# Top-32 attention and two MLPs on one core: both heads' masks on ScalarE in the first 20 attention steps, with a new set of order priorities

## The chip, the cores and the metric

One core of one Trainium2 chip runs the whole program. The metric is the device time of one execution, in microseconds. The kernel before has a median of 669.65 us over three runs (668.49 to 670.56). The engines are called PE (TensorE, the matmuls), PEld (TensorE's weight loads), DVE (VectorE), ACT (ScalarE), POOL (GpSimd) and SP (SyncE, which issues every DMA here).

## The reference, cut to what matters

```python
def _attn_ref(q, k, v):                  # q, k, v: (2, 8, 576, 64)
    scores = scale * np.matmul(q, k.transpose(0, 1, 3, 2))
    kth = np.partition(scores, -32, axis=-1)[..., -32:-31]
    scores = np.where(scores >= kth, scores, -1e9)
    scores = scores - np.max(scores, axis=-1, keepdims=True)
    attn = np.exp(scores)
    attn = attn / (np.sum(attn, axis=-1, keepdims=True) + 1e-09)
    return np.matmul(attn, v)

def _moe_ref(x, w_in, w_out):            # x: (1152, 512), d_ff 2048
    h = x @ w_in
    return (h * np.tanh(softplus(h))) @ w_out

def _moe2_ref(x, w_a, w_b, w_out):       # d_ff 1536
    return ((x @ w_a) * (x @ w_b)) @ w_out
```

The attention's output (1152 tokens by 512) goes through the first MLP and that through the second. Of each row of 576 scores only those that reach the 32nd largest count.

## The kernel before, in words

**Tiles and steps.** The 1152 tokens are nine tiles of 128, t = 0 to 8. Attention takes a tile in four steps (`hp` = 0 to 3, two heads each), 36 steps in all, in the order t, hp. Step number 4t + hp runs through these lines:

- `scores` (L405): q is split into two fp32r parts (`cast` L338, `minus` L343), PE multiplies (L420), and ACT scales the result into the score tile `s2` (L425).
- `largest` (L429): four rounds on DVE for each of the two heads. Each round finds the next eight largest values of 576 (MAX8, L439), and all but the last strike them out (MATCH_REPLACE8, L443). POOL makes `nm`, minus the largest value, after round one (L448).
- `weighted_sum` (L452): the masked exponentials `e2` and their row sums `sm`. The two heads go two ways. Head 0: ACT takes exp(score + nm) (L464), and DVE multiplies that by score >= kth with one SCALAR_TENSOR_TENSOR that also gives the row sum (L467). Head 1: POOL forms `dm` = kth + nm (L471), ACT takes a Prelu of kth - score with slope 2 to the -100 below zero (L474), and ACT takes exp of minus 2 to the 100 times that plus `dm`, with the row sum (L477); what lies below kth comes out as zero.
- PE transposes `e2` in three groups of three (L487), ACT copies them (L338), PE multiplies by v (L499, L503), and ACT copies the result.
- In a tile's last step (hp = 3) the row sums are inverted (L514, L516), spread by PE (L522), and multiplied in by DVE (L528). That gives the tile's `X`.

**MLPs.** `SEQ` (L26) gives their order: the first MLP for tile 0, 1 and 2 alone with f32 matmuls, the second MLP for tiles 0 to 2 together, then first and second for tiles 3 to 5, and first and second for tiles 6 to 8, with operands split in two fp32r parts. In `gated` (first MLP, L642) PE makes a block of h (L595), DVE and ACT make the gate (L670, L675, L678), PE accumulates (L616, L618). In `bilinear` (second MLP, L709) ACT copies one product, DVE multiplies (L725), PE accumulates (L618).

**Weights.** The weights come as 64-bit words in 68 units. Each unit is loaded, turned to fp32 by two ACT instructions (L546, L549) and two POOL instructions (L556, L560), stored to DRAM (`ws`) and read again by later users (`weight`, L567).

**Order.** Every operation is added to a `Plan` (L62) with the engines that may run it, a cost in ns and a priority. `Plan.run` (L108) is a list scheduler: it steps through its own clock, and each engine takes the ready operation of the lowest priority number whose buffers are free. The program is then emitted in that order, so on the chip each engine has a fixed order of instructions. The priority numbers come from tables: `ATT` (a knot for each attention tile), `CONV` (weights), `MLP` (a pair for each entry of `SEQ`) and `BIAS` (an offset for each kind of operation). Casts may go to ACT or DVE and subtractions to POOL or DVE (`SHIFT` adds to an engine's priority for them); `LOCKED` charges an operation for waiting on a lock that the planner assumes between DVE and POOL.

Of the kernel before, what the change touches and what calls it, by code (L numbers as in the profile page):

```python
# [9 lines left out]
F32 = mybir.dt.float32  # L10
F32R = mybir.dt.float32r
I32 = mybir.dt.int32
U32 = mybir.dt.uint32
AF = mybir.ActivationFunctionType
ALU = mybir.AluOpType
# [3 lines left out]
P = 128  # L19
U = 512  # L20
TOPK = 32
F1, F2 = 16, 12
NEG = -3.0e38
STEEP = 2.0 ** 100

SEQ = [(1, (0,), 0), (1, (1,), 0), (1, (2,), 0), (2, (0, 1, 2), 1), (1, (3, 4, 5), 1), (2, (3, 4, 5), 1),  # L26
       (1, (6, 7, 8), 1), (2, (6, 7, 8), 1)]
ATT = (-44.2, 61.0, 80.2, 153.1, 238.0, 259.3, 281.3, 398.4, 274.4, 469.0)
CONV = (-27.3, 62.1, 145.7, 238.5, 305.1)
MLP = ((99.9, 149.6), (74.9, 213.2), (116.2, 202.1), (235.2, 335.9), (398.3, 83.3), (374.8, 661.3), (641.9, 1133.6),  # L30
        (636.8, 878.2))
BIAS = {'scores': -33.7, 'search': 20.5, 'weigh': 16.8, 'gate': -247.0, 'conv': 3.7, 'load': -25.3, 'split': -20.8,
        'x': -50.1, 'k': -24.9, 'prod': -14.5, 'acc': 7.3, 'out': -497.1, 'store': 13.6, 'v': 290.8, 'px': 5.6,
        'mask': 2.0, 'turn': -2.6}
FRESH = 200
KEEP = (1, 1, 1, 1, 1, 3, 3, 3)
AHEAD = 1500.0
SLACK = 2500.0
ISSUE = 430.0
TICK = 3413.0  # L40
DUTY = 0.375
SPARE = (6000.0, 4000.0, 3000.0, 2000.0, 1000.0, 500.0, 0.0)
# [219 lines left out]


LAG = {"PE": 200.0, "DVE": 135.0, "ACT": 150.0, "POOL": 110.0, "SP": 2200.0}
SHIFT = {'DVE': 20.6, 'POOL': -2.0, 'ACT': 198.1, 'PE': 0, 'SP': 0}
LOCKED = 85.8


def ramp(knots, z):
# [6 lines left out]
def topk_attention_mlps(ctx: ExitStack, tc: tile.TileContext, q, k, v, vr, w, out):  # L276
# [5 lines left out]

    nc = tc.nc
    B, D, H, S = k.shape
    DM = H * D
    NC = DM // P
    NP = H // 2
    J = 4
    SM = J * P
    R = S - SM  # L290
# [8 lines left out]
    add = plan.add  # L299
# [3 lines left out]
    def buf(pool, shape, dtype, name, cap=1):  # L303
        if pool == "dp":
            return plan.buf(lambda b: pools[pool].tile(shape, dtype, name=name), None, 0)
        n = (8 if dtype == mybir.dt.int64 else 4)
        for z in shape[1:]:
            n *= z

        def make(b):  # L310
            a = arena[b.kind][:shape[0], b.at // 4:(b.at + n) // 4]
            if dtype != b.kind:
                a = a.bitcast(dtype)
            if len(shape) > 2:
                dims = "abcde"[:len(shape) - 1]
                a = a.rearrange(f"p ({' '.join(dims)}) -> p {' '.join(dims)}", **dict(zip(dims, shape[1:])))
            return a
        b = plan.buf(make, None if pool == "const" else f"{pool}.{name}", cap)
        b.size, b.kind, b.name = -(-n // 32) * 32, F32R if dtype == F32R else F32, name
        return b  # L320
# [7 lines left out]
    def one(engine, cost, locks=False):  # L328
        return {engine: (cost, locks)}
# [23 lines left out]
    nc.vector.memset(eight, 8)  # L353
    nc.scalar.preload_act_table_set("natural_log_exp_and_others")

    V, V4, KK, QQ, X, XR, Y = {}, {}, {}, {}, {}, {}, {}

    def groups(t):
        return [(t // (J + 1), 0, P)] if t != J else [(b, b * R, R) for b in range(B)]
# [66 lines left out]
                    [(psc, 0)], [(s2, (s, a))])  # L426
        return s2

    def largest(s2, at):  # L429
        pr = at + BIAS["search"]  # L430
        wk, m8 = buf("att", [P, 2, S], F32, "wk", CAPS["wk"]), buf("att", [P, 2, TOPK], F32, "m8", 2)
        nm = buf("att", [P, 2], F32, "nm", 2)
        for r in range(TOPK // 8):
            for s in range(2):
                src = wk if r else s2
                keys = [(wk, s)] if r else [(s2, (s, a)) for a in range(2)]
                got = slice(8 * r, 8 * r + 8)
                add(one("DVE", 672.0), pr,
                    lambda e, s=s, src=src, got=got: nc.vector.max(m8()[:, s, got], src()[:, s, :]),  # L439
                    keys, [(m8, (s, r))])  # L440
                if r < TOPK // 8 - 1:
                    add(one("DVE", 680.0), pr,
                        lambda e, s=s, src=src, got=got: nc.vector.match_replace(wk()[:, s, :], m8()[:, s, got],  # L443
                                                                                src()[:, s, :], NEG),
                        keys + [(m8, (s, r))], [(wk, s)])
            if r == 0:
                add(one("POOL", 174.0), pr,
                    lambda e: nc.gpsimd.tensor_scalar(nm(), m8()[:, :, 0], -1.0, None, op0=ALU.mult),  # L448
                    [(m8, (0, 0)), (m8, (1, 0))], [(nm, 0)])
        return m8, nm  # L450

    def weighted_sum(t, hp, at, s2, m8, nm):  # L452
        pr = at + BIAS["weigh"]
        if hp == 0:
            if t in (0, J):
                load_v(t // J, pr + BIAS["v"])
            XR[t] = buf("att", [P, NP, P], F32, "xr", 2), buf("att", [P, H], F32, "sm", 2)
        xr, sm = XR[t]
# [1 line left out]
        last = TOPK // 8 - 1  # L460
        kth = lambda s: m8()[:, s, TOPK - 1:TOPK]
        at_ = lambda s: sm()[:, 2 * hp + s:2 * hp + s + 1]
        s0, s1 = ([(s2, (s, a)) for a in range(2)] for s in range(2))
        add(one("ACT", 665.0), pr, lambda e: nc.scalar.activation(e2()[:, 0, :], s2()[:, 0, :], AF.Exp,  # L464
                                                                bias=nm()[:, 0:1]), s0 + [(nm, 0)], [(e2, 0)])
        add(one("DVE", 740.0, True), pr + BIAS["mask"],
            lambda e: nc.vector.scalar_tensor_tensor(e2()[:, 0, :], s2()[:, 0, :], kth(0), e2()[:, 0, :],  # L467
                                                   op0=ALU.is_ge, op1=ALU.mult, accum_out=at_(0)),
            s0 + [(m8, (0, last)), (e2, 0)], [(e2, 0), (sm, (hp, 0))])
        dm = buf("att", [P, 1], F32, "dm", 2)  # L470
        add(one("POOL", 142.0), pr, lambda e: nc.gpsimd.tensor_add(dm(), kth(1), nm()[:, 1:2]),  # L471
            [(m8, (1, last)), (nm, 0)], [(dm, 0)])
        add(one("ACT", 665.0), pr,
            lambda e: nc.scalar.activation(e2()[:, 1, :], s2()[:, 1, :], AF.Prelu, scale=-1.0, bias=kth(1),  # L474
                                           alpha=1.0 / STEEP), s1 + [(m8, (1, last))], [(e2, 1)])
        add(one("ACT", 775.0), pr,
            lambda e: nc.scalar.activation(e2()[:, 1, :], e2()[:, 1, :], AF.Exp, scale=-STEEP, bias=dm(),  # L477
                                           accum_out=at_(1)), [(e2, 1), (dm, 0)], [(e2, 1), (sm, (hp, 1))])
        et = buf("att", [P, 2 * J + 1, P], F32, "et", CAPS["et"])
        for g in range(3):  # L480
            pe = bank("pe")
# [50 lines left out]
    for t, hp in steps:  # L532
        at = ATT[t] + (ATT[t + 1] - ATT[t]) * hp / NP
        s2 = scores(t, hp, at)
        weighted_sum(t, hp, at, s2, *largest(s2, at))

    order = [(z, f, i) for z, F in ((0, F1), (1, F2)) for f in range(F) for i in range(2 + z)]
    stored, fresh = {}, {}
# [100 lines left out]
            add(one("DVE", 600.0), pr, lambda e: nc.vector.tensor_sub(put(yl), src(), put(yh).bitcast(F32)),  # L639
                read + [(yh, i)], [(yl, i)])  # L640

    def gated(z, tiles, split, yt, places, direct):  # L642
        n = len(tiles)
        T = n * P
        base = lambda f: MLP[z][0] + (MLP[z][1] - MLP[z][0]) * f / F1
# [6 lines left out]
            xz = [((X[tiles[0]], 0), lambda c: X[tiles[0]]()[:, c, :])]  # L652
        acc = [bank("acc", "ps_a") for _ in tiles]
        if direct:
            acc.append(bank("acc"))
        K = WIDE.get(T, 1)
        for f0 in range(0, F1, K):
            ph = bank("ph", "ps_h")
# [24 lines left out]
                add_product(base(f0 + j), acc, gj, wb, n, f0 + j == 0, f0 + j == F1 - 1, direct)  # L683
        pr = base(F1)
        if direct:
            for c in range(NC):
                put = lambda y, c=c: y()[:, c, :]
                add(one("ACT", 75.0 + 0.83 * T), pr + BIAS["x"],
                    lambda e, c=c, put=put: nc.scalar.mul(put(yt[0]), acc[c]()[:, :T], -1.0), [(acc[c], 0)],
                    [(yt[0], c)])  # L690
                add(one("DVE", 65.0 + 1.04 * T), pr + BIAS["x"],
                    lambda e, c=c, put=put: nc.vector.scalar_tensor_tensor(
                        put(yt[1]), acc[c]()[:, :T], -1.0, put(yt[0]).bitcast(F32), op0=ALU.mult, op1=ALU.subtract),
                    [(acc[c], 0), (yt[0], c)], [(yt[1], c)])
            return
        for i in range(n):
            y = buf("xp", [P, DM], F32, "y")
            add(one("ACT", 495.0), pr + BIAS["x"], lambda e, y=y, i=i: nc.scalar.mul(y(), acc[i](), -1.0),
                [(acc[i], 0)], [(y, 0)])
            pt = bank("pt")  # L700

            def turn(e, y=y, pt=pt):
                for c in range(NC):
                    nc.tensor.transpose(pt()[:, c * P:(c + 1) * P], y()[:, c * P:(c + 1) * P], ident)

            add(one("PE", 440.0), pr + BIAS["x"], turn, [(y, 0)], [(pt, 0)])
            parted(pr, lambda pt=pt: pt().rearrange("p (c t) -> p c t", t=P), [(pt, 0)], yt, places[i], False)

    def bilinear(z, tiles, yt):  # L709
        n = len(tiles)  # L710
# [30 lines left out]
    for i, (kind, tiles, split) in enumerate(SEQ):  # L741
        if kind == 2:
            bilinear(i, tiles, Y[tiles[0]][0])
            continue
        if tiles[0] not in Y:
            group = next(z[1] for z in SEQ if z[0] == 2 and tiles[0] in z[1])
            yt = [buf("xp", [P, NC, len(group) * P], F32R, f"y{z}{len(group) * P}", CAPS["y"]) for z in "hl"]
            Y.update({t: (yt, j) for j, t in enumerate(group)})
        whole = any(z[0] == 2 and z[1] == tiles for z in SEQ)
        gated(i, tiles, split, Y[tiles[0]][0], [Y[t][1] for t in tiles], i == final and split and whole)  # L750

    started = plan.run()
    plan.place(started, ROOM)
# [49 lines left out]
```

## Time and profile before

| what | value |
|---|---|
| median of three runs | 669.65 us (668.49 to 670.56) |
| the profiled execution's own time | 669.99 us |
| its span, from first to last instruction | 668.2 us |
| PE busy | 612.0 us, 92% of the span |
| PEld busy | 538.5 us, 81% |
| DVE busy | 583.8 us, 87% |
| ACT busy | 479.6 us, 72% |
| POOL busy | 403.6 us, 60% |
| mean granted TensorE clock | 0.977 of full speed |

The shares are averages over stages that differ. The profile lists the busy time of each engine in stretches of the span, the chain of work that ended last, each line's instructions with their mean duration, and who waited for whom. PE's busy time is modelled, so a busy PE need not be a PE at its peak.

### The profile page before, as it was taken

The page shows a single profiled execution, that of the slowest core. Times are in us where ns is not written, and L with a number is a line of the kernel's source. Part 1 is how long each engine was busy: PE and PEld are TensorE (multiplying, and loading weights), DVE is VectorE, ACT ScalarE, POOL GpSimd, SP SyncE. Part 2 cuts the span into 40 slices and gives each one's busy share as a digit, 9 for nine tenths or more (in the row PEclk, how much of TensorE's full clock was granted, in tenths as well). Part 3 has the DMA queues.
Part 4 walks back from the last instruction along what each step waited for, and adds up shares of the span by engine and source line. Part 5 has one row for each costly group of instructions (what it writes and reads, how often), then busy time and mean ns, then how long its engine had stood idle before and what let it go on. Part 6 is the DMA issues. An engine that isn't in the chain of part 4 may idle for free.

```text
span 668.2 us, 12021 instructions
## 1 busy us (share of the span) xinstructions
PE 612.0 (92%) x4000; PEld 538.5 (81%) x4000; DVE 583.8 (87%) x1141; ACT 479.6 (72%) x1040; POOL 403.6 (60%) x417
## 2 busy tenths in 40 slices
PE   1567987799989999999999999899999999999997
PEld 1455965677775989887799998899899999999997
DVE  4999999999999999999999999999973676675661
ACT  4789988869878798989799876766663687632222
POOL 5898867457559899999987656375631122321220
PEclk9958998999999999999999999999999999999999
DMA  9978886996999968777564433232304544444401
GB/s 268 301 246 266 223 258 162 339 337 202 336 334 285 304 191 267 239 229 242 177 199 145 127 103 118 80 80 80 110 1 150 182 136 134 126 127 127 128 14 47
DMA packets 55869, 123.99 MB, mean 186 GB/s; under 512 B 7424, under 2 KB 7424, under 8 KB 55808
## 3 DMA queue, kind: packets, MB, share of 16 engines
q1 hardware_dynamic: 55808, 123.23, 59.6%
q8 instruction: 31, 0.51, 0.3%
q14 instruction: 30, 0.25, 0.1%
HBM read 103.02 MB, written 20.19 MB: 184 GB/s over the span
## 4 chain that ended last, share of the span: by engine, by line
PE 54%; DVE 18%; DMA 4%; ACT 3%; POOL 3%; issue 3%; SPq 0%; DVEq 0%; POOLq 0%; ACTq 0%
PE ph L595 28%; PE po L618 8%; DVE arena L439 7%; PE acc L618 5%; DVE arena L443 5%; PE acc L616 5%; PE px L499 3%; DMA arena<-ws 2%; PE pe L487 2%; PE psc L420 2%; DMA ws<-arena 2%; POOL arena L560 1%; DVE arena L467 1%; DVE arena L343 1%; ACT arena L338 1%
## 5 line engine op out<-in xcount | busy, mean ns | idle before, releaser
L343 POOL TENSOR_TENSOR arena<-arena,arena 128x512 fp32r<-128x512 f32 (+4 forms) x186 | 217.8, 1183 | 178.4 <-ACT arena L338 155.6
L595 PE MATMUL ph<-arena 128*128 128x384 f32 (+1 forms) x1632 | 284.5, 324 | 8.2 <-POOL arena L560 4.8
L595 PEld LDWEIGHTS ph<-arena 128*128 128x128 f32 x1632 | 264.1, 189 | 24.0 <-issue 10.3
L439 DVE MAX8 arena<-arena 128x8 f32<-128x576 f32 x288 | 204.7, 746 | 0.7 <-ACT arena L425 0.7
L338 ACT CAST arena<-arena 128x384 fp32r<-128x384 f32 (+4 forms) x225 | 121.0, 560 | 54.8 <-DVE arena L725 36.2
L443 DVE MATCH_REPLACE8 arena<-arena 128x576 f32<-128x576 f32 x216 | 159.2, 741 | 0.0
L343 DVE TENSOR_TENSOR arena<-arena,arena 128x512 fp32r<-128x512 f32 (+4 forms) x116 | 92.5, 797 | 6.1 <-ACT arena L338 4.1
L675 ACT ACTIVATE arena<-arena 128x384 f32<-128x384 f32 (+1 forms) x132 | 73.0, 555 | 32.7 <-DVE arena L670 31.6
L560 POOL TENSOR_TENSOR arena<-arena 128x512 int32<-128x512 int32 x68 | 90.2, 1327 | 9.5 <-PE psc L420 1.8
L556 POOL TENSOR_TENSOR arena<-arena,eight 128x512 uint32<-128x512 uint32 x67 | 75.0, 1122 | 27.2 <-ACT arena L546 21.4
L420 PE MATMUL psc<-arena 128*128 128x288 f32 x320 | 66.1, 333 | 25.8 <-POOL arena L343 13.3
L618 PE MATMUL acc<-arena 128*128 128x512 f32 x240 | 86.0, 483 | 3.0 <-DVE arena L678 3.0
L618 PE MATMUL po<-arena 128*128 128x512 f32 x324 | 81.5, 396 | 0.0
L420 PEld LDWEIGHTS psc<-arena 128*128 128x128 f32 x320 | 50.8, 202 | 36.5 <-POOL arena L343 16.1
L618 PEld LDWEIGHTS po<-arena 128*128 128x128 f32 x324 | 59.2, 188 | 11.4 <-ACT arena L338 0.2
L338 ACT COPY arena<-pe 128x384 f32<-128x384 f32 x108 | 48.9, 490 | 20.0 <-PE pe L487 19.3
L487 PE MATMUL pe<-ident,arena 128*128 128x128 f32 x324 | 50.5, 290 | 12.1 <-DVE arena L467 7.4
L487 PEld LDWEIGHTS pe<-ident,arena 128*128 128x128 f32 x324 | 40.9, 149 | 25.2 <-DVE arena L467 7.0
L425 ACT ACTIVATE arena<-psc 128x288 f32<-128x288 f32 x144 | 53.5, 422 | 10.0 <-PE psc L420 9.7
L725 DVE TENSOR_TENSOR arena<-ph,arena 128x384 f32<-128x384 f32 x36 | 19.8, 550 | 40.3 <-PE ph L595 40.1
L618 PEld LDWEIGHTS acc<-arena 128*128 128x128 f32 x240 | 42.3, 192 | 13.4 <-issue 4.1
L338 ACT COPY arena<-ph 128x384 f32<-128x384 f32 x36 | 17.3, 480 | 44.1 <-PE ph L595 44.1
(48 smaller groups left out, 638.3 us busy)
## 6 DMA issues: line engine op xcount, KB each, us to landing
arena<-ws SPq DMA_DIRECT2D x212, 256.0 KB, 3.0
arena<-in_w_dram SPq DMA_DIRECT2D x68, 512.0 KB, 4.9
ws<-arena SPq DMA_DIRECT2D x68, 256.0 KB, 4.6
arena<-in_q_dram SPq DMA_DIRECT2D x18, 256.0 KB, 5.4
arena<-in_k_dram SPq DMA_DIRECT2D x16, 288.0 KB, 6.3
arena<-in_v_dram SPq DMA_DIRECT2D x4, 512.0 KB, 7.4
out_dram<-arena SPq DMA_DIRECT2D x8, 256.0 KB, 2.4
arena<-in_vr_dram SPq DMA_DIRECT2D x4, 64.0 KB, 6.4
```

The source lines that it names most:

```text
L338: add(eng, prio, lambda e: nc.scalar.copy(dst(), src()) if e == "ACT" else nc.vector.tensor_copy(dst(), src()), reads, writes)
L343: lambda e: ENG[e].tensor_sub(dst(), a(), b()), reads, writes)
L420: nc.tensor.matmul(psc()[:, :HS], z()[:, s, :], kk()[:, a * HS:(a + 1) * HS], start=(i == 0), stop=(i == len(heads) - 1))
L425: lambda e, s=s, a=a, psc=psc: nc.scalar.mul(s2()[:, s, a * HS:(a + 1) * HS], psc()[:, :HS], SCALE),
L439: lambda e, s=s, src=src, got=got: nc.vector.max(m8()[:, s, got], src()[:, s, :]),
L443: lambda e, s=s, src=src, got=got: nc.vector.match_replace(wk()[:, s, :], m8()[:, s, got], src()[:, s, :], NEG),
L487: nc.tensor.transpose(pe()[:, i * P:(i + 1) * P], ef[:, n * P:(n + 1) * P], ident)
L556: nc.gpsimd.tensor_tensor(wi().bitcast(U32), wi().bitcast(U32), eight.to_broadcast([P, U]), op=ALU.mult)
L560: lambda e, word=word, wi=wi: nc.gpsimd.tensor_tensor(wi(), wi(), word(I32, 0), op=ALU.add),
L595: nc.tensor.matmul(ph()[:, o:o + T], a, x, start=(i == 0), stop=(i == len(mm) - 1))
L618: nc.tensor.matmul(acc[i](), z[:, i * P:(i + 1) * P], a, start=begin, stop=end)
L675: lambda _, dst=dst, e=e, fn=fn, kw=kw: nc.scalar.activation(dst(), e(), fn, **kw),
```

## The change

Steps with 4t + hp < `MASK` = 20, all of tiles 0 to 4, take head 0 the way of head 1. In them the exponential of L464 and the DVE instruction of L467 fall away, and a Prelu and an exponential with row sum on ACT are added for head 0. POOL's `dm` becomes one instruction for both heads. Steps 20 to 35 keep one head on DVE. The tables `ATT`, `CONV`, `MLP`, `BIAS`, `SHIFT` and `LOCKED` have new numbers, and two new offsets, `tail` and `last`, are added to the priority of the weighted sum and of the search in a tile's last step. So the planner makes a new order for all engines.

The core of the diff (`...` marks what is left out):

```diff
-ATT = (-44.2, 61.0, 80.2, 153.1, 238.0, 259.3, 281.3, 398.4, 274.4, 469.0)
-CONV = (-27.3, 62.1, 145.7, 238.5, 305.1)
-MLP = ((99.9, 149.6), (74.9, 213.2), (116.2, 202.1), (235.2, 335.9), (398.3, 83.3), (374.8, 661.3), (641.9, 1133.6),
-        (636.8, 878.2))
-BIAS = {'scores': -33.7, 'search': 20.5, 'weigh': 16.8, 'gate': -247.0, 'conv': 3.7, 'load': -25.3, 'split': -20.8,
...
+ATT = (-97.3, 58.3, 77.3, 151.4, 260.3, 261.3, 311.1, 456.8, 390.8, 840.0)
+CONV = (-69.4, 19.3, 161.8, 256.3, 308.6)
+MLP = ((104.1, 136.2), (63.5, 241.3), (69.4, 197.1), (259.1, 368.8), (592.8, 89.5), (744.4, 1618.1), (1185.6,
+        1061.3), (552.5, 642.6))
+BIAS = {'scores': -35.7, 'search': 51.6, 'weigh': 16.4, 'gate': -435.3, 'conv': 1.1, 'load': -0.3, 'split': -21.2,
+        'x': -216.4, 'k': -20.5, 'prod': -4.5, 'acc': 6.4, 'out': -120.8, 'store': 27.4, 'v': 308.4, 'px': -12.5,
+        'mask': -73.8, 'turn': -10.7, 'tail': -0.7, 'last': 0.7}
...
+MASK = 20
...
-SHIFT = {'DVE': 20.6, 'POOL': -2.0, 'ACT': 198.1, 'PE': 0, 'SP': 0}
-LOCKED = 85.8
+SHIFT = {'DVE': 24.4, 'POOL': 4.8, 'ACT': 603.0, 'PE': 0, 'SP': 0}
+LOCKED = 141.4
...
-    def largest(s2, at):
-        pr = at + BIAS["search"]
+    def largest(s2, hp, at):
+        pr = at + BIAS["search"] + (BIAS["last"] if hp == NP - 1 else 0.0)
...
-        pr = at + BIAS["weigh"]
+        pr = at + BIAS["weigh"] + (BIAS["tail"] if hp == NP - 1 else 0.0)
...
+        n = 2 if 4 * t + hp < MASK else 1
+        if n == 1:
+            add(one("ACT", 665.0), pr, lambda e: nc.scalar.activation(e2()[:, 0, :], s2()[:, 0, :], AF.Exp,
+                                                                    bias=nm()[:, 0:1]), src[0] + [(nm, 0)], [(e2, 0)])
+            add(one("DVE", 740.0, True), pr + BIAS["mask"],
+                lambda e: nc.vector.scalar_tensor_tensor(e2()[:, 0, :], s2()[:, 0, :], kth(0), e2()[:, 0, :],
+                                                       op0=ALU.is_ge, op1=ALU.mult, accum_out=at_(0)),
+                src[0] + [(m8, (0, last)), (e2, 0)], [(e2, 0), (sm, (hp, 0))])
+        dm = buf("att", [P, n], F32, f"dm{n}", 2)
+        add(one("POOL", 142.0), pr,
+            lambda e: nc.gpsimd.tensor_add(dm(), m8()[:, 2 - n:, TOPK - 1], nm()[:, 2 - n:]),
+            [(m8, (s, last)) for s in range(2 - n, 2)] + [(nm, 0)], [(dm, 0)])
+        for s in range(2 - n, 2):
+            add(one("ACT", 665.0), pr,
+                lambda e, s=s: nc.scalar.activation(e2()[:, s, :], s2()[:, s, :], AF.Prelu, scale=-1.0, bias=kth(s),
+                                                    alpha=1.0 / STEEP), src[s] + [(m8, (s, last))], [(e2, s)])
+            add(one("ACT", 775.0), pr,
+                lambda e, s=s: nc.scalar.activation(e2()[:, s, :], e2()[:, s, :], AF.Exp, scale=-STEEP,
+                                                    bias=dm()[:, s - 2 + n:s - 1 + n], accum_out=at_(s)),
+                [(e2, s), (dm, 0)], [(e2, s), (sm, (hp, s))])
...
-            acc.append(bank("acc"))
+            acc += [bank("acc", "ps_a") for _ in range(CAPS["acc"] - n)] + [bank("acc")]
```

The last pair, and a changed way of handing the output tiles to `gated`, give the same buffers as before: `CAPS["acc"]` is 3, and the groups have three tiles. The new constant `ENTRY` is read nowhere.

## Rows read from the trace of the kernel before

**Rows 1.** Windows: stretch, its us, busy us (instructions) by engine, PE clock, DMA share, GB/s

```profile
0.00:25.00 25.00, 4.89 (x16) 3.90 (x16) 16.06 (x34) 13.09 (x25) 15.95 (x22) 1.00 0.96 298
25.00:100.00 75.00, 59.85 (x411) 48.83 (x411) 75.00 (x157) 67.82 (x155) 64.22 (x67) 0.84 0.81 247
100.00:200.00 100.00, 90.01 (x631) 68.48 (x632) 98.58 (x200) 80.44 (x172) 60.21 (x75) 0.97 0.86 285
200.00:275.00 75.00, 73.46 (x513) 63.82 (x512) 74.77 (x145) 64.77 (x149) 71.31 (x73) 1.00 0.85 258
275.00:421.00 146.00, 140.82 (x951) 124.57 (x949) 144.94 (x290) 122.24 (x271) 114.84 (x108) 1.00 0.56 173
421.00:524.00 103.00, 102.33 (x712) 93.57 (x713) 86.14 (x174) 62.33 (x139) 46.96 (x48) 1.00 0.29 88
524.00:669.00 145.00, 140.68 (x772) 135.30 (x770) 88.34 (x148) 68.94 (x138) 30.11 (x27) 1.00 0.37 109
```

**Rows 2.** Chain that ended last, in order of time: start us, us, what

```profile
421.58 2.38 PE ph L595 x12
...
660.55 4.13 PE po L618 x18
```

**Rows 3.** L528 on DVE, each tile's end: duration ns min/median/max, first and last start

```profile
L528 DVE TENSOR_TENSOR arena<-arena,prs x9: 661/671/690, 68.9 to 508.4; 128x512 f32<-128x512 f32 x9
```

**Rows 4.** Windows of L467 alone: us, DVE busy (instructions), clock, DMA share

```profile
25.00:100.00 75.00, 7.52 (x14) 0.84 0.81 247
100.00:200.00 100.00, 7.00 (x16) 0.97 0.86 285
200.00:275.00 75.00, 5.92 (x9) 1.00 0.85 258
```

**Rows 5.** L467 by itself: duration ns min/median/max

```profile
L467 DVE SCALAR_TENSOR_TENSOR arena<-arena x36: 792/812/1944, 24.7 to 492.2; 128x576 f32<-128x576 f32 x36
```

**Rows 6.** ACT groups, 0 to 275 us: count | busy us, mean ns | idle before

```profile
L464 ACT ACTIVATE arena<-arena 128x576 f32<-128x576 f32 x20 | 15.9, 795 | 1.2 <-POOL arena L448 1.2
L477 ACT ACTIVATE arena<-arena 128x576 f32<-128x576 f32 x20 | 15.7, 787 | 0.1
L474 ACT ACTIVATE arena<-arena 128x576 f32<-128x576 f32 x20 | 15.7, 787 | 6.7 <-DVE arena L439 6.7
...
L477 ACT ACTIVATION_READ_ACCUMULATOR arena<-arena 128x1 f32 x20 | 4.2, 209 | 0.0
```

**Rows 7.** ACT groups, 25 to 100 us: the casts of q and k

```profile
L338 ACT CAST arena<-arena 128x256 fp32r<-128x256 f32 x9 | 3.6, 428 | 0.0
...
L338 ACT CAST arena<-arena 128x576 fp32r<-128x576 f32 x2 | 1.4, 687 | 0.0
```

**Rows 8.** The same casts on DVE, whole span

```profile
L338 DVE CAST arena<-arena 128x576 fp32r<-128x576 f32 x8 | 4.4, 554 | 1.9 <-DMA arena<-in_k_dram 1.9
...
L338 DVE CAST arena<-arena 128x256 fp32r<-128x256 f32 x6 | 2.1, 348 | 4.8 <-DMA arena<-in_q_dram 4.8
```

**Rows 9.** PE's waits, 0 to 200 us: us in total, times, longest

```profile
PE pe L487 <- DVE arena L467: 5.7, 4, 2.6
PE ph L595 <- POOL arena L560: 4.8, 4, 1.9
...
PE pe L487 <- ACT arena L477: 4.7, 2, 3.2
```

**Rows 10.** Timeline at tile 0's last step: start us, us, what [idle before]

```profile
56.42 0.74 DVE L439 MAX8 arena<-arena 128x8 f32<-128x576 f32 x1
...
58.98 0.92 ACT L474 ACTIVATE arena<-arena 128x576 f32<-128x576 f32 x1
...
60.29 0.84 ACT L546 ACTIVATE arena<-arena 128x512 f32<-128x512 f32 x1
...
61.41 0.93 ACT L477 ACTIVATE arena<-arena 128x576 f32<-128x576 f32 x1
...
62.49 1.33 PE L487 MATMUL pe<-ident,arena 128*128 128x128 f32 x5 [3.17 <-ACT arena L477]
```

More of the change, by code (lines that the diff above doesn't have):

```diff
@@ L27 @@
        (1, (6, 7, 8), 1), (2, (6, 7, 8), 1)]
-ATT = (-44.2, 61.0, 80.2, 153.1, 238.0, 259.3, 281.3, 398.4, 274.4, 469.0)
-CONV = (-27.3, 62.1, 145.7, 238.5, 305.1)
-MLP = ((99.9, 149.6), (74.9, 213.2), (116.2, 202.1), (235.2, 335.9), (398.3, 83.3), (374.8, 661.3), (641.9, 1133.6),
-        (636.8, 878.2))
-BIAS = {'scores': -33.7, 'search': 20.5, 'weigh': 16.8, 'gate': -247.0, 'conv': 3.7, 'load': -25.3, 'split': -20.8,
-        'x': -50.1, 'k': -24.9, 'prod': -14.5, 'acc': 7.3, 'out': -497.1, 'store': 13.6, 'v': 290.8, 'px': 5.6,
-        'mask': 2.0, 'turn': -2.6}
+ATT = (-97.3, 58.3, 77.3, 151.4, 260.3, 261.3, 311.1, 456.8, 390.8, 840.0)
[5 more added lines that the diff above has]
+        'mask': -73.8, 'turn': -10.7, 'tail': -0.7, 'last': 0.7}
 FRESH = 200
@@ L38 @@
 SLACK = 2500.0
+MASK = 20
 ISSUE = 430.0
+ENTRY = 100.0
 TICK = 3413.0
@@ L284, in topk_attention_mlps @@
     B, D, H, S = k.shape
+    NP = H // 2
     DM = H * D
     NC = DM // P
-    NP = H // 2
     J = 4
@@ L354, in topk_attention_mlps @@
     nc.scalar.preload_act_table_set("natural_log_exp_and_others")
-    V, V4, KK, QQ, X, XR, Y = {}, {}, {}, {}, {}, {}, {}
+    V, V4, KK, QQ, QS, X, XR, Y = {}, {}, {}, {}, {}, {}, {}, {}
     def groups(t):
@@ L462, in weighted_sum @@
         at_ = lambda s: sm()[:, 2 * hp + s:2 * hp + s + 1]
[L463 to L478, printed above, removed]
+        src = [[(s2, (s, a)) for a in range(2)] for s in range(2)]
@@ L534, in topk_attention_mlps @@
         s2 = scores(t, hp, at)
-        weighted_sum(t, hp, at, s2, *largest(s2, at))
+        weighted_sum(t, hp, at, s2, *largest(s2, hp, at))
     order = [(z, f, i) for z, F in ((0, F1), (1, F2)) for f in range(F) for i in range(2 + z)]
@@ L640, in parted, with gated @@
                 read + [(yh, i)], [(yl, i)])
-    def gated(z, tiles, split, yt, places, direct):
+    def gated(z, tiles, split, ys, direct):
         n = len(tiles)
@@ L685, in gated @@
         if direct:
+            yt = ys[0][0]
             for c in range(NC):
@@ L706, in gated @@
             add(one("PE", 440.0), pr + BIAS["x"], turn, [(y, 0)], [(pt, 0)])
-            parted(pr, lambda pt=pt: pt().rearrange("p (c t) -> p c t", t=P), [(pt, 0)], yt, places[i], False)
+            parted(pr, lambda pt=pt: pt().rearrange("p (c t) -> p c t", t=P), [(pt, 0)], *ys[i], False)
     def bilinear(z, tiles, yt):
@@ L744, in topk_attention_mlps @@
             continue
[L745 to L748, printed above, removed]
+        for t in tiles:
+            if t not in Y:
+                group = next(z[1] for z in SEQ if z[0] == 2 and t in z[1])
+                yt = [buf("xp", [P, NC, len(group) * P], F32R, f"y{z}{len(group) * P}", CAPS["y"]) for z in "hl"]
+                Y.update({t: (yt, j) for j, t in enumerate(group)})
         whole = any(z[0] == 2 and z[1] == tiles for z in SEQ)
-        gated(i, tiles, split, Y[tiles[0]][0], [Y[t][1] for t in tiles], i == final and split and whole)
+        gated(i, tiles, split, [Y[t] for t in tiles], i == final and split and whole)
     started = plan.run()
```

## The prediction

> **What bounds the kernel now.** I read the stages first, then the chain, then the lines that the edit touches. The windows by stage [rows 1] show a change of bound. From 25 to 275 us DVE is busy 248.4 of 250 us (75.00 + 98.58 + 74.77) while PE still has gaps and, up to 200 us, a lowered clock. From 275 to 421 us DVE (144.94) and PE (140.82 of 146) are both full. From 524 us DVE is at 61% and PE at 97%. The chain of waits [rows 2] agrees: from 421.58 us to the last matmuls at 660.55 us hardly anything but PE stands on it. PE's work is the same in both kernels, so the end comes earlier only by what PE loses less before 421 us. That loss lies at the front: PE idles for 20.1 us in the first 25 us, 15.2 in 25 to 100, 10.0 in 100 to 200, and only 6.7 from there to 421 us [rows 1]. What sets the front is when the tiles come out of attention, the first at 68.9 us and the last at 508.4 us [rows 3], and a tile's steps go through a DVE queue that is never empty. So a microsecond taken off DVE in the first 275 us can be worth a microsecond at the end, if no other engine takes over. The 20 steps of the change are just these: their mask instructions lie in the first 275 us [rows 4].
>
> **What DVE loses.** L467 occupies DVE for 7.52, 7.00 and 5.92 us in the three stages, 20.4 us in all, its accumulator reads included; these are 7, 8 and 5 steps, counted by their mask instructions [rows 4]. None of this lies beside other DVE work.
>
> **What ACT gains.** For each of the 20 steps one exponential (795 ns) goes, and a Prelu (787), an exponential (787) and an accumulator read (209) come: +988 ns, 19.8 us in all [rows 6]. Head 1 already takes this road between exponentials, so the durations need no guess. By stages the 19.8 us are 6.9, 7.9 and 4.9. ACT is idle for 7.2, 19.6 and 10.2 us there [rows 1]. So ACT has a cover, but a thin one in the first stage; without it the 19.8 us come on the path one for one.
>
> **Stage 25 to 100 us.** DVE falls to 67.5 us, ACT rises to 74.7. Casts may change engines: those of q and k hold 5.0 us of ACT here [rows 7] and are shorter on DVE, 348 for 428 ns and 554 for 687 [rows 8], so about 4.1 us. With all of them moved DVE has 71.6 and ACT 69.7 us of work. The saving lies between 0.3 us (nothing moved, ACT full) and 3.4 us (all moved, DVE full). I take 2, since both engines would then be at 95% or more, which DVE now holds but ACT (90%) does not quite.
>
> **Stage 100 to 200 us.** DVE falls from 98.6 to 91.6, ACT rises from 80.4 to 88.3. The saving is at most 7.0 us. ACT would be at 95% of 93 us, the DMA engines go from 0.86 to about 0.92, and PE already waits for converted weights (L560, 4.8 us) [rows 9]. I take 4.5.
>
> **Stage 200 to 275 us.** DVE falls by 5.9 us, ACT rises to 69.7 of 75, but POOL is at 71.3 of 75, which leaves 3.7 us unless subtractions go to DVE. I take 2.5, with 0 and 5.9 as ends.
>
> L467 is longer where POOL is fuller: 0.88 us a step with POOL at 60%, 1.18 with POOL at 95% [rows 1, 4], and it reaches 1944 ns from a least of 792 [rows 5]. The Trainium skill, "SBUF — State Buffer", section "SBUF: two separate sides", says that DVE with two SBUF inputs and POOL exclude each other for a whole instruction, so POOL would get time back too. By that rule the last stage would save all of its 5.9 us and the sum would be 12.4 instead of 9.
>
> **What costs nothing.** POOL's `dm` stays one instruction a step; it now waits for both heads' last search, and behind it in POOL's queue stand conversions and subtractions, but it starts on the same MAX8 as before, which was the later of the two. The buffers and PE's instructions are the same. The offsets `tail` and `last` are under a nanosecond of the planner's priority.
>
> **The new order.** The trace cannot show it. It may move any load, conversion or cast past others in the queues of SP, POOL, ACT and DVE. From the nearest rows: PE's waits for converted weights (4.8 us) and for the masks (5.7 + 4.7 us) are 15.2 us up to 200 us [rows 9]; a better order could remove them, a worse one double them. I take 0, and keep plus and minus 8 (half of it) for the range: nothing says that all of them go one way.
>
> **Sum.** 2 + 4.5 + 2.5 = 9.0 us. The rest of the span, which DVE and then PE fill, moves forward as it is. Against the profiled execution's own 669.99 us (1.8 more than its span) this gives 661.0. The median of the runs shown is 669.65, 0.3 below that execution, which changes nothing at this size: 661.0 us.
>
> **The rivals.**
>
> *All of DVE's time comes back.* If casts and subtractions are shared so that ACT and POOL never hold DVE up, the front is 20.4 us shorter: 649.6 us. For it: DVE is full throughout [rows 1]. Against it: ACT's 74.7 in the first stage, POOL's 71.3 in the last.
>
> *The gain is absorbed.* ACT takes DVE's place in the first stage (0.3 us saved), and weights, conversion and DMA hold the rest: about 669 us. For it: DMA at 0.81 to 0.86, ACT and POOL together near full [rows 1]. Against it: in 100 to 200 us POOL has 40 us left.
>
> *Slower: ACT's queue at the end of a step.* Before, only head 1's Prelu, exponential and read follow the last search; afterwards both heads' do, 1.78 us more before the last transposes. In tile 0's last step the search is over at 57.16 us, the Prelu starts at 58.98, a conversion at 60.29 lies before the exponential at 61.41, and PE has stood still for 3.17 us when it goes on at 62.49 [rows 10]. So ACT's queue, not the mask, already sets this wait. Up to 200 us PE waits six times for masks (four for L467, two for L477) [rows 9]. If each grows by the full 1.78 us, that is 10.7 us; with nothing saved in the first stage, 7.0 us of the sum are left: 669.99 + 10.7 - 7.0 = 673.7. It decides from 1.5 us a wait (9.0 over six), so only if ACT hides almost nothing. Against it: later steps give PE other work.
>
> In 25 to 100 us the granted clock averages 0.84 of full speed, so 24 of the 75 us went at 1.2 GHz, the rest at 2.4 [rows 1]. The Trainium skill, "TensorE: Matmul & The Clock Gate", section "What's actually happening", says that the low clock is the default and activity releases it. By that rule longer waits would also cost clock: with a fall from 0.84 to 0.78 in this stage the slower case would be at some 678 us. I give this a third of that case's chance.
>
> That the change does not do what it says can be left out: the mask instructions are either in the program or not.
>
> **How the numbers follow.** Forecast, 655 to 666 us, centre 661: 0.52. Nearly all of DVE's time, 646 to 655: 0.13. Absorbed, 666 to 671.7: 0.20, of which 0.08 below 667.6. Slower, 671.7 to 680: 0.15. About 0.3% (2.0 us) can be told from no change here, so faster is below 667.6: 0.52 + 0.13 + 0.08 = 0.73; same 0.12; slower 0.15. The range runs from 651 (the stages' upper ends, 3.4 + 7.0 + 5.9, give 653.7, and a better order some of its 8) to 671 (absorbed, 669, with an order a little worse). It leaves out the slower case and the lower part of the second, about 0.19.
>
> **What would show it.** After: 16 instructions of L467's kind on DVE and 20 more pairs on ACT; DVE's sum down by 20 to 22 us, ACT's up by about 20, less what casts move. The first three tiles' ends come earlier by about 1, 4 and 7 us, and the first stretch in which PE stays full begins some 9 us sooner. ACT's waits for DVE shrink and DVE begins to wait for ACT's score copies (L425). The prediction is wrong if DVE shows gaps before 275 us that are as large as what it lost, if PE's waits for the last transposes grow past 1.5 us each, or if the stretch from 275 to 421 us, which I move forward unchanged, changes its length by more than the front does.

## The result and the profile after

The changed kernel takes 662.89 us (median of four runs, 662.48 to 663.90) against 670.07 us for the kernel before in the same runs: a ratio of 0.9899, 95% interval 0.9885 to 0.9913, or 7.2 us. The forecast was 661.0. The profiled execution took 663.90 us with a span of 662.1, so it is 6.1 us under the profiled execution of before. It is the slowest of the four and has the lowest mean clock: 663.90 us at 0.973, 662.96 and 662.83 at 0.979, 662.48 at 0.985.

The windows by stage of the changed kernel, same stretches and columns as [rows 1]:

```profile
0.00:25.00 25.00, 4.89 (x16) 3.90 (x16) 16.39 (x35) 12.88 (x26) 14.01 (x20) 1.00 0.95 298
25.00:100.00 75.00, 57.87 (x381) 47.05 (x382) 74.81 (x153) 68.93 (x157) 58.17 (x62) 0.80 0.80 239
100.00:200.00 100.00, 94.80 (x696) 72.75 (x695) 98.40 (x201) 93.60 (x204) 59.95 (x78) 0.98 0.90 296
200.00:275.00 75.00, 72.95 (x536) 63.19 (x535) 73.05 (x146) 70.81 (x161) 68.99 (x73) 1.00 0.90 288
275.00:421.00 146.00, 143.57 (x973) 128.05 (x975) 142.28 (x282) 126.78 (x288) 110.77 (x105) 1.00 0.50 152
421.00:524.00 103.00, 102.97 (x674) 94.17 (x673) 86.29 (x167) 59.22 (x127) 42.77 (x43) 1.00 0.33 101
```

PE's idle time is a stretch's length less its first busy number (the stretch from 524 us to the end, left out here, has 3.5 us of it before and 4.0 after). Against [rows 1] it goes from 20.1 to 20.1 us in the first stretch, from 15.2 to 17.1 in 25 to 100 us (with the clock down from 0.84 to 0.80), from 10.0 to 5.2 in 100 to 200, from 1.5 to 2.1 in 200 to 275, from 5.2 to 2.4 in 275 to 421, and from 0.7 to nothing in 421 to 524. That is 5.7 us less idle time up to 524 us, of the 6.1 us between the two profiled executions. So the gain sits in 100 to 200 and in 275 to 421 us, and the first stage, where the sum of the prediction had 2 us of gain, is worse.

DVE is as full as before up to 200 us, and 1.7 and 2.7 us emptier in the two stretches after that. The groups of DVE from 0 to 275 us show what it does with the time that the masks left; before (count | busy us, mean ns | idle before):

```profile
L439 DVE MAX8 arena<-arena 128x8 f32<-128x576 f32 x167 | 118.1, 746 | 0.7 <-ACT arena L425 0.7
L443 DVE MATCH_REPLACE8 arena<-arena 128x576 f32<-128x576 f32 x125 | 92.1, 742 | 0.0
...
L343 DVE TENSOR_TENSOR arena<-arena,arena 64x576 fp32r<-64x576 f32 x6 | 5.5, 922 | 0.2
...
L554 DVE TENSOR_SCALAR arena<-arena 128x512 int32<-128x512 int32 x1 | 1.0, 1001 | 0.6 <-ACT arena L546 0.6
```

and after, where L561 is the line that L554 was (one half of a weight's conversion, which POOL or DVE may take), and L345 is L343:

```profile
L441 DVE MAX8 arena<-arena 128x8 f32<-128x576 f32 x173 | 122.4, 746 | 0.8 <-ACT arena L427 0.7
L445 DVE MATCH_REPLACE8 arena<-arena 128x576 f32<-128x576 f32 x130 | 95.9, 742 | 0.0
...
L345 DVE TENSOR_TENSOR arena<-arena,arena 64x576 fp32r<-64x576 f32 x8 | 8.6, 1070 | 0.5 <-ACT arena L340 0.3
...
L561 DVE TENSOR_SCALAR arena<-arena 128x512 int32<-128x512 int32 x10 | 6.4, 642 | 0.6 <-ACT arena L553 0.6
```

Of the 20.4 us of [rows 4], 8.1 went into more search by 275 us (4.3 + 3.8), and 8.5 into conversions and k's subtractions, most of which POOL did before (5.4 + 3.1). POOL's total falls from 403.6 to 382.1 us. ACT's groups from 0 to 275 us are as priced from [rows 6]:

```profile
L483 ACT ACTIVATE arena<-arena 128x576 f32<-128x576 f32 x41 | 31.9, 781 | 0.0
L480 ACT ACTIVATE arena<-arena 128x576 f32<-128x576 f32 x41 | 31.7, 783 | 3.6 <-DVE arena L441 3.5
L483 ACT ACTIVATION_READ_ACCUMULATOR arena<-arena 128x1 f32 x41 | 8.3, 202 | 0.0
```

The first tile leaves attention later than before, the last one 19.5 us sooner (68.9 and 508.4 us in [rows 3]):

```profile
L535 DVE TENSOR_TENSOR arena<-arena,prs x9: 660/680/689, 73.4 to 488.9; 128x512 f32<-128x512 f32 x9
```

The second, third and fourth tile, before (start us, us):

```profile
114.44 0.68 DVE L528 TENSOR_TENSOR arena<-arena,prs 128x512 f32<-128x512 f32 x1
160.52 0.68 DVE L528 TENSOR_TENSOR arena<-arena,prs 128x512 f32<-128x512 f32 x1
255.85 0.67 DVE L528 TENSOR_TENSOR arena<-arena,prs 128x512 f32<-128x512 f32 x1
```

and after:

```profile
115.08 0.67 DVE L535 TENSOR_TENSOR arena<-arena,prs 128x512 f32<-128x512 f32 x1
158.03 0.69 DVE L535 TENSOR_TENSOR arena<-arena,prs 128x512 f32<-128x512 f32 x1
213.90 0.69 DVE L535 TENSOR_TENSOR arena<-arena,prs 128x512 f32<-128x512 f32 x1
```

The first three come 4.5 us later, 0.6 later and 2.5 sooner, the fourth 42 us sooner. So the new order does not only shift the old one forward: from the fourth tile on every tile comes 11 to 47 us sooner, and the end comes only some 6 us sooner.

How far the search has come is read from the windows of the MAX8 line alone (us, DVE busy with the count, clock, DMA share, GB/s). Before:

```profile
0.00:100.00 100.00, 43.74 (x62) 0.88 0.85 260
100.00:200.00 100.00, 43.95 (x63) 0.97 0.86 285
```

and after:

```profile
0.00:100.00 100.00, 43.72 (x62) 0.85 0.84 254
100.00:200.00 100.00, 48.77 (x70) 0.98 0.90 296
```

A step has eight MAX8. Up to 100 us the search is no further than before; from 100 to 200 us it does seven more, nearly a step.

### The profile page after: what moved, and what is told of

It is laid out like the page before. It is cut to its first block, busy times and chain, and to the rows that moved or that the text cites. A ratio compares the mean times of both kernels' runs of the same rounds, so it can differ in the third digit from the quotient of the medians.

```text
span 662.1 us, 12033 instructions
## 1 busy us (share of the span) xinstructions
PE 611.1 (92%) x4000; PEld 537.5 (81%) x4000; DVE 575.8 (87%) x1118; ACT 493.3 (74%) x1077; POOL 382.1 (58%) x403
## 4 chain that ended last, share of the span: by engine, by line
PE 52%; DVE 5%; ACT 4%; issue 2%; POOL 1%; DMA 1%; SPq 0%; DVEq 0%; POOLq 0%; ACTq 0%
PE ph L602 27%; PE po L625 9%; PE acc L623 5%; PE acc L625 3%; PE px L506 3%; PE pe L494 2%; PE psc L422 2%; DVE arena L445 2%; DVE arena L441 2%; ACT arena L340 1%; POOL arena L345 1%; ACT arena L682 1%; PE prs L529 1%; DMA arena<-ws 1%; PE px L510 1%
## 5 line engine op out<-in xcount | busy, mean ns | idle before, releaser
L345 POOL TENSOR_TENSOR arena<-arena,arena 128x512 fp32r<-128x512 f32 (+4 forms) x183 | 211.8, 1169 | 188.8 <-ACT arena L340 172.1
L340 ACT CAST arena<-arena 128x512 fp32r<-128x512 f32 (+4 forms) x222 | 120.6, 566 | 50.2 <-DVE arena L733 32.0
L345 DVE TENSOR_TENSOR arena<-arena,arena 128x512 fp32r<-128x512 f32 (+4 forms) x119 | 99.9, 841 | 5.2 <-ACT arena L340 3.3
L567 POOL TENSOR_TENSOR arena<-arena 128x512 int32<-128x512 int32 x68 | 88.9, 1310 | 10.3 <-issue 1.9
L422 PE MATMUL psc<-arena 128*128 128x288 f32 x320 | 69.3, 340 | 27.5 <-DVE arena L345 13.3
L563 POOL TENSOR_TENSOR arena<-arena,eight 128x512 uint32<-128x512 uint32 x56 | 59.6, 1068 | 30.0 <-ACT arena L553 29.7
L427 ACT ACTIVATE arena<-psc 128x288 f32<-128x288 f32 x144 | 54.4, 415 | 10.8 <-PE psc L422 10.2
L494 PEld LDWEIGHTS pe<-ident,arena 128*128 128x128 f32 x324 | 41.0, 150 | 21.4 <-ACT arena L483 12.7
L480 ACT ACTIVATE arena<-arena 128x576 f32<-128x576 f32 x56 | 43.3, 781 | 13.4 <-DVE arena L441 13.3
```

The costliest lines, as they stand in the source:

```text
L340: add(eng, prio, lambda e: nc.scalar.copy(dst(), src()) if e == "ACT" else nc.vector.tensor_copy(dst(), src()), reads, writes)
L345: lambda e: ENG[e].tensor_sub(dst(), a(), b()), reads, writes)
L422: nc.tensor.matmul(psc()[:, :HS], z()[:, s, :], kk()[:, a * HS:(a + 1) * HS], start=(i == 0), stop=(i == len(heads) - 1))
L427: lambda e, s=s, a=a, psc=psc: nc.scalar.mul(s2()[:, s, a * HS:(a + 1) * HS], psc()[:, :HS], SCALE),
L494: nc.tensor.transpose(pe()[:, i * P:(i + 1) * P], ef[:, n * P:(n + 1) * P], ident)
L563: nc.gpsimd.tensor_tensor(wi().bitcast(U32), wi().bitcast(U32), eight.to_broadcast([P, U]), op=ALU.mult)
```

## The experiments

Two theories stood against each other. LOADS (also called DVE below) is the sum of the prediction: the gain is the work that goes from a full DVE to an ACT with room. ORDER: the work that moves is worth little or nothing by itself, and the gain is in how all the instructions are ordered. In five kernels the order was held fixed on every engine, so that only loads and dependences change: their traces list the same instructions in the same order on each engine, but for the edited ones. Medians are beside the kernel before in the same runs (669.3 to 669.7 us).

### DVE lighter, order of before

In the first 20 steps DVE's mask covers 8 of 576 columns, so row sums and masking of head 0 are left out there.

```diff
+        w = 8 if 4 * t + hp < 20 else S
-            lambda e: nc.vector.scalar_tensor_tensor(e2()[:, 0, :], s2()[:, 0, :], kth(0), e2()[:, 0, :],
+            lambda e: nc.vector.scalar_tensor_tensor(e2()[:, 0, :w], s2()[:, 0, :w], kth(0), e2()[:, 0, :w],
```

> The order of the kernel before, unchanged; in the first 20 steps DVE's mask works on 8 of 576 columns, so the row sums and the masking of head 0 are left out there and DVE loses some 18 us (20 x (1.05 - 0.1)) while ACT gets nothing. Theory DVE (DVE's queue sets the front, what it loses comes off the end): 652 to 661 us. Theory ORDER (the gain of the change comes from its new tables, not from DVE's time): within 2 us of before, 668 to 672.

662.62 us, ratio 0.9912 (0.9885 to 0.9939): 7.0 us faster. The group of the short masks from 0 to 275 us, and the first full stage (columns as in [rows 1]):

```profile
L468 DVE SCALAR_TENSOR_TENSOR arena<-arena 128x8 f32<-128x8 f32 x20 | 8.8, 440 | 0.0
```

```profile
25.00:100.00 75.00, 61.84 (x420) 50.24 (x419) 74.46 (x161) 70.21 (x161) 61.46 (x67) 0.98 0.82 251
```

A mask of 8 columns still takes 440 ns on average, so DVE lost 12.3 us (20 x (1.054 - 0.440), where 1.054 us is the mean of the 20 full ones) and not 18. Seven of the 12.3 came off the end, which lies between the two expectations. DVE's time does set a part of the front, as the prediction said: by 275 us the search has 172 MAX8 behind it instead of 167. PE's clock is 0.98 in this stage for 0.84; PE's busy time for the same work falls by 1.5 us over the whole span (612.0 to 610.5), which is what the higher clock can have given directly.

The 20 short masks took from 0.20 to 1.13 us. A long one, with the POOL instruction beside it:

```profile
44.53 1.28 POOL L561 TENSOR_TENSOR arena<-arena 128x512 int32<-128x512 int32 x1
44.71 1.13 DVE L468 SCALAR_TENSOR_TENSOR arena<-arena 128x8 f32<-128x8 f32 x1
```

and a short one, with no POOL instruction beside it:

```profile
157.67 0.20 DVE L468 SCALAR_TENSOR_TENSOR arena<-arena 128x8 f32<-128x8 f32 x1
```

The long one ends at 45.84 us, POOL's at 45.81. So it is with the twelve masks of 0.25 us and more: each ends 0.02 to 0.03 us after a TENSOR_TENSOR of POOL. The other eight took 0.20 to 0.24 us.

### ACT heavier, order of before

```diff
+            if 4 * t + hp < 20:
+                nc.scalar.activation(e2()[:, 0, :], s2()[:, 0, :], AF.Exp, bias=nm()[:, 0:1], accum_out=junk())
             nc.scalar.activation(e2()[:, 0, :], s2()[:, 0, :], AF.Exp, bias=nm()[:, 0:1])
```

> The order of the kernel before, with one more exponential with row sum on ACT (about 0.99 us) ahead of head 0's exponential in the first 20 steps; the result is not changed. Theory DVE with a full ACT in the first stage: 25 to 100 us has 7.2 us idle on ACT for 6.9 us more, so the front gets later by 3 to 8 us: 673 to 678. Theory that ACT has room: 669 to 672.

677.51 us, ratio 1.0127 (1.0091 to 1.0163): 7.9 us slower, as the theory of a full ACT expected. The windows of the first two full stages:

```profile
25.00:100.00 75.00, 58.71 (x397) 47.67 (x399) 73.74 (x153) 69.83 (x162) 62.06 (x65) 0.91 0.75 229
100.00:200.00 100.00, 89.31 (x627) 68.61 (x623) 95.57 (x195) 84.95 (x183) 59.00 (x73) 0.95 0.85 281
```

But ACT is not full: it never gets past 69.8 of 75 us and 85.0 of 100, yet DVE falls to 95.6 of 100 us where it had 98.6 [rows 1], and PE follows. So ACT's idle time covered about 12 of the 20 us that were added and not the other 7.9, although 5 to 15 us of it were left in each stage: in a fixed order an instruction that comes late on ACT holds up those behind it. The added exponential stands in front of head 0's mask here, not behind the last search as in the change.

### Both loads, order of before

The two diffs above together.

> Both of the two other edits at once in the order of the kernel before: DVE is 18 us lighter, ACT 20 us heavier, as in the change (masking and sums of head 0 left out in the first 20 steps). Theory DVE: the two effects add up, 660 to 667. Theory ORDER: 668 to 674, since an order made for the old loads cannot use them.

671.74 us, ratio 1.0031 (1.0017 to 1.0045): 2.1 us slower. Added up, the two effects are 0.9 us slower (7.9 - 7.0); together they are a little worse. The time is in the range of ORDER. The effects do add up, nearly, but to no gain, and the 660 to 667 us of LOADS is ruled out for loads alone in this order.

### The true swap, order of before

Head 0's exponential goes in the first 20 steps; at the place of DVE's mask stand a small add on POOL and the two ACT instructions. This adds 20 small POOL instructions that the changed kernel does not have.

```diff
+            nc.gpsimd.tensor_add(d0(), kth(0), nm()[:, 0:1])
+            nc.scalar.activation(e2()[:, 0, :], s2()[:, 0, :], AF.Prelu, scale=-1.0, bias=kth(0), alpha=1.0 / STEEP)
+            nc.scalar.activation(e2()[:, 0, :], e2()[:, 0, :], AF.Exp, scale=-STEEP, bias=d0(), accum_out=at_(0))
```

> The order of the kernel before, held fixed on every engine; only in the first 20 steps head 0's exponential is dropped and, where DVE's mask stood, POOL's small add, a Prelu and an exponential with row sum stand on ACT. Theory LOADS (the swap of work between DVE and ACT is the gain, as the sum of the prediction has it): 659 to 666. Theory ORDER (the swap alone is worth nothing, DVE's relief and ACT's load cancel as in the two load experiments, and the longer chain after the last search comes on top): 670 to 680.

683.1 us, ratio 1.0183 (1.0117 to 1.0248): 13.4 us slower, slower than both expectations, and 11.3 slower than the two loads alone. The POOL adds are not free: ACT waited 3.1 us for them in all, so a part of the 11.3 can be theirs. The waits of PE from 0 to 200 us (us in total, times, longest) with the two loads, where L484 is head 1's second ACT instruction and L474 DVE's mask:

```profile
PE pe L494 <- ACT arena L484: 8.3, 5, 3.3
...
PE pe L494 <- DVE arena L474: 2.0, 1, 2.0
```

and with the swap, where L478 is head 0's second ACT instruction and L490 head 1's:

```profile
PE pe L500 <- ACT arena L478: 11.1, 9, 3.7
PE pe L500 <- ACT arena L490: 10.3, 6, 3.5
```

PE waits for masks for 21.4 us where it was 10.4 in the kernel before [rows 9] and 10.3 with the two loads: 11.0 us more than before. PE's idle time of every kind grows by less up to 200 us, from 45.2 to 50.8 us, since other waits shrink. The timeline of the swap at tile 0's last step:

```profile
56.78 1.42 DVE L439 MAX8 arena<-arena 128x8 f32<-128x576 f32 x2
...
61.55 0.78 ACT L478 ACTIVATE arena<-arena 128x576 f32<-128x576 f32 x1
...
63.19 0.78 ACT L487 ACTIVATE arena<-arena 128x576 f32<-128x576 f32 x1
...
65.61 0.80 ACT L490 ACTIVATE arena<-arena 128x576 f32<-128x576 f32 x1
...
66.55 1.33 PE L500 MATMUL pe<-ident,arena 128*128 128x128 f32 x5 [3.43 <-ACT arena L490]
```

The second pair of ACT instructions stands behind the first, with a score copy and a conversion between its two halves, and PE starts the last transposes at 66.55 us instead of 62.49 [rows 10]. Of these 4.1 us 1.0 was there when the search ended (58.20 for 57.16), and 3.0 came behind it. That is the slower rival of the prediction, in its place. In the changed kernel the same transposes start as late as in the swap:

```profile
66.17 1.33 PE L494 MATMUL pe<-ident,arena 128*128 128x128 f32 x5 [1.99 <-ACT arena L483]
```

PE stood idle for 1.99 us before them, not 3.43. So in this step the new order does not make the longer chain shorter; it gives PE other work in the meantime.

### The old masks, order of the changed kernel

The reverse: in the first 20 steps an exponential stands where head 0's Prelu stood, and DVE's mask takes the place of its second exponential in the order.

```diff
+                if n == 2 and s == 0:
+                    nc.scalar.activation(e2()[:, 0, :], s2()[:, 0, :], AF.Exp, bias=nm()[:, 0:1])
...
+                    nc.vector.scalar_tensor_tensor(e2()[:, 0, :], s2()[:, 0, :], kth(0), e2()[:, 0, :],
+                                                   op0=ALU.is_ge, op1=ALU.mult, accum_out=at_(0))
```

> The order of the changed kernel, held fixed; in the first 20 steps an exponential with nm stands where head 0's Prelu stood, and DVE's mask goes into DVE's queue where head 0's second exponential stood. Theory LOADS: the gain is gone and no more, 668 to 673. Theory ORDER (an order fits the loads that it was made for): 673 to 685.

682.99 us, ratio 1.0175 (1.0121 to 1.0229): 13.3 us slower than before and 20.1 slower than the changed kernel. That is within what ORDER expected. In both directions the swap at a fixed order costs, 13 us one way and 20 the other. Each order fits the loads for which it was made.

### Masks without the new tables, tables without the masks

> Both heads' masks on ACT in the first 20 steps with the priority tables of the kernel before (the two new offsets at zero); the planner makes its order with them. Theory DVE: 661 to 667, most of the gain is there without new tables. Theory ORDER: 668 to 676, the gain is not there without them.

684.1 us, ratio 1.0207 (1.0165 to 1.0249).

```diff
-MASK = 20
+MASK = 0
```

> The changed kernel's tables with MASK at 0: every step keeps one head's mask on DVE. Theory DVE: without DVE's 20 us there is no gain, 668 to 677. Theory ORDER: most of the gain, 661 to 666.

681.8 us, ratio 1.0182 (1.0152 to 1.0211). Neither half gives any of the gain; each costs more than 12 us, and both times lie above every range that was expected. So the new tables alone are not the gain either, as ORDER had it here: it takes the masks and the tables together. The planner made a new order in each case, so these two say nothing of loads by themselves, as the next ones show.

### One offset moved by 1.0

The work is the same; the planner's priority offset of the score products is moved by plus or minus 1.0, in the kernel before (-33.7) and in the changed one (-35.7).

> The kernel before with the priority offset of the score products moved by 1.0 (-33.7 to -32.7), nothing else; the planner makes its order anew. Theory ORDER: the same work in a neighbouring order is slower by 3 to 12 us, 673 to 682. Theory LOADS (orders of the same work differ little): 668 to 671.

> The kernel before with the offset of the score products moved the other way, by -1.0 (-33.7 to -34.7). Theory ORDER (the tables of before are a point with one especially good order, most orders near it are worse): 675 to 683, as with +1.0. Rival (the slow neighbour was an accident of that one step): 668 to 672.

> The changed kernel with the same offset moved by 1.0 (-35.7 to -34.7). Theory ORDER: 661 to 672, slower than the changed kernel by up to 9 us or equal. Theory LOADS: 661 to 664.

> The changed kernel with the same offset moved by -1.0 (-35.7 to -36.7). Theory ORDER: 667 to 676, several us slower than the changed kernel, and with +1.0 (665.8) the neighbours of the changed kernel are together faster than those of the kernel before by about as much as the two kernels differ, or more. Rival (the changed kernel owes its time to its loads): 661 to 665.

| offset | kernel before | changed kernel |
|---|---|---|
| as it is | 669.7 | 662.9 |
| +1.0 | 680.9, ratio 1.0144 (1.0088 to 1.0200) | 665.8, ratio 0.9936 (0.9909 to 0.9964) |
| -1.0 | 682.0, ratio 1.0145 (1.0068 to 1.0223) | 673.6, ratio 1.0061 (1.0029 to 1.0093) |

All ratios are to the kernel before. A priority number moved by 1.0, with no instruction added or taken away, costs the kernel before 11 to 12 us and the changed one 3 to 11, all four within what ORDER expected. The windows of 421 to 524 us for before with +1.0, and of 200 to 275 us for the changed kernel with -1.0, show a part of it:

```profile
421.00:524.00 103.00, 99.22 (x685) 89.64 (x684) 84.68 (x168) 57.68 (x128) 44.98 (x48) 0.98 0.29 91
```

```profile
200.00:275.00 75.00, 69.67 (x492) 60.20 (x491) 72.54 (x136) 64.04 (x143) 64.97 (x70) 0.95 0.88 276
```

In the first PE loses 3.1 us and clock where it was full before (102.33 [rows 1]); in the second 3.3 us against the changed kernel (72.95), with ACT and POOL emptier too.

### Both heads on ACT from step 7 only

```diff
-        n = 2 if 4 * t + hp < MASK else 1
+        n = 2 if 7 <= 4 * t + hp < MASK else 1
```

> The changed kernel, but the first 7 steps (those whose masks lie before 100 us) keep head 0 on DVE; steps 7 to 19 have both heads on ACT. Theory that ACT is too full in the first stage (PE lost 2.7 us more there than before): 658 to 662, faster than the changed kernel by 1 to 4 us. Rival, that DVE's time in the first 7 steps is worth as much as later: 665 to 668, slower than the changed kernel by 2 to 5 us.

667.42 us, ratio 0.9972 (0.9956 to 0.9988): 4.5 us slower than the changed kernel, within what the rival expected. (By the windows of the result PE was busy 2.0 us less in that stage than before, not 2.7.) But the order is another one here too, and a neighbouring order alone can cost 3 to 11 us, so this does not tell the first seven steps' worth.

## Why the prediction came out right, and where its steps did not

**The time** came out inside the range, 1.9 us from the forecast. **Its sum did not come about in the way that it was worked out.** That the two numbers lie so near is in good part luck. The 9.0 us was the net of two loads, DVE relieved and ACT covered, with the new order at zero. Measured at the old order, the two loads net to 2.1 us slower, and the swap itself to 13.4 us slower. From there to the changed kernel are 20.2 us (683.1 to 662.9), which only the new order can have given, apart from the 20 small POOL adds. By the other way round, the new order costs 13.3 us with the old masks, and the swap in it saves 20.1. So neither has a price of its own; it depends on the other. The step that failed is "The new order. I take 0", with 8 us either way, as a term beside the loads: the order decides what the loads are worth, and a nudge alone, the same work in another order, moved the kernel before by 11.3 and 12.3 us. The two offsets `tail` and `last`, 0.7 each, were put at nothing as "under a nanosecond"; they are in the planner's own numbers, not in time, and 1.0 of another offset was worth 3 to 12 us. What these two are worth no run shows.

**What DVE loses** was right in size, 20.4 us, and right in that it pays: 12.3 us taken off DVE gave 7.0. But it did not show as a loss of DVE work. DVE's total fell by 8.0 us (583.8 to 575.8), not by 20 to 22, since the new order gave it conversions and subtractions from POOL.

**What ACT gains** was right in size (988 ns a step), and its cover was half right. The prediction read 7.2, 19.6 and 10.2 us of idle time as room. In the order of before some 20 us more cost 7.9 us, though ACT kept 5 to 15 us of idle time in each stage; about 12 us were covered. ACT's total grew by 13.7 us in the changed kernel (479.6 to 493.3).

**The stages.** PE's idle time changed by +1.9 us in 25 to 100 (2 us of gain forecast), by -4.8 in 100 to 200 (4.5 of gain forecast), by +0.5 in 200 to 275 (2.5 of gain forecast), and by -2.8 in 275 to 421 (unchanged in the forecast). So the second stage came as forecast, the first and third did not, and the fourth made up for a part of that. Of the tests that the prediction set itself, the first three tiles should have come sooner by about 1, 4 and 7 us; they came 4.5 later, 0.6 later and 2.5 sooner. And by PE's idle time the stretch from 275 to 421 us, moved forward unchanged in the prediction, changed by 2.8 us, more than all of 0 to 275 us (2.3 less): one of its own signs of being wrong. DVE's wait for ACT's score copies up to 275 us stayed at 0.7 us.

**The slower rival** was priced with 10.7 us for six waits of 1.78. In the old order PE's waits for masks grow by 11.0 us, and the swap is 11.3 us slower than the loads alone. So the mechanism was right for that order, and the sum of the waits too, but not the way to it: there are fifteen such waits of 1.4 us in the mean, not six of longer ones. Nor does 11.0 explain 11.3 by itself, since PE's idle time of every kind grew by 5.6 us up to 200 us. The time, 683.1 us, is above the 671.7 to 680 of this rival. That it did not come true is the new order's doing: PE's waits for masks up to 200 us are 8.9 us in the changed kernel, less than the 10.4 of before:

```profile
PE pe L494 <- ACT arena L483: 8.9, 5, 2.4
PE acc L625 <- DVE arena L685: 2.6, 3, 1.8
PE ph L602 <- POOL arena L567: 1.7, 1, 1.7
```

The wait for converted weights (L567, L560 before) is 1.7 us for 4.8 [rows 9], which agrees with the conversions that DVE took.

**The two rules that the prediction cited.** The Trainium skill, "SBUF — State Buffer", section "SBUF: two separate sides", says that DVE with two SBUF inputs and POOL exclude each other for a whole instruction. The short masks agree: with two inputs of 8 columns each they end 0.02 to 0.03 us after POOL's instruction in the twelve long cases, up to 1.13 us, and take 0.20 to 0.24 us in the others. That the third stage would save all of its 5.9 us, which the prediction worked out from it, did not come: PE's idle time grew by 0.5 us there, and POOL's busy time fell by 2.3 (71.31 to 68.99). The Trainium skill, "TensorE: Matmul & The Clock Gate", section "What's actually happening", says that the low clock is the default and activity releases it. In 25 to 100 us PE's idle time and clock go together at the ends, 13.2 us at 0.98 (lighter DVE), 15.2 at 0.84 (before), 17.1 at 0.80 (after) and 24.1 at 0.77 (old masks in the new order), and not between, 16.3 at 0.91 (heavier ACT), 19.0 at 0.89 (new tables without the masks) and 20.0 at 0.82 (the swap). So the idle time in sum does not give the clock. The swap's windows of that stage:

```profile
25.00:100.00 75.00, 55.03 (x365) 44.39 (x366) 64.19 (x132) 68.44 (x157) 57.24 (x68) 0.82 0.71 219
```

It also shows DVE at 64.2 of 75 us, less than in any other kernel here: the queue that was never empty has gaps there.

**What stays open.** Four orders that the planner made for the old masks and four that it made for the new ones were run. They do not show whether the old masks, in the best order for them, could be as fast as the changed kernel. The kernel before is the fastest of the old-mask orders that were run (669.7, then 680.9, 681.8, 682.0), and the changed one the fastest with the new masks (662.9, then 665.8, 673.6, 684.1). That the new masks allow better orders is what these suggest, and it is not shown. Nor do the runs tell which of the instructions that the new order moved matter.

## What to carry to other kernels

In a kernel whose instructions stand in a planned order, a change of loads and a change of order cannot be priced apart: hold the order fixed and move the loads, in the old order and in the new one, and allow for the new order at least what a nudge of one priority costs. Idle time of an engine with a fixed order is room only in part: here about 12 of 20 us. When work moves to an engine that stands behind the last result of a step, count the longer chain at its end in the waits that are there already, as was done here for the rival, and ask whether the new order can hide it.

## What the runs showed of the hardware

A DVE mask with row sum over 8 columns took 440 ns on average, against 1054 ns over 576 columns in the kernel before. Twelve of the 20 short ones end 0.02 to 0.03 us after a POOL instruction and took up to 1127 ns; the eight others took 200 to 239 ns. So the time that such a mask shows depends above all on the POOL instruction beside it.

TensorE's mean granted clock in one stage (25 to 100 us) ran from 0.77 to 0.98 of full speed over the kernels here, whose PE did 325 to 420 matmuls there. The changed kernel's own four executions followed their mean clock, from 663.90 us at 0.973 to 662.48 at 0.985; those of the kernel before did not (669.94 at 0.990, 668.49 at 0.978).
